# Writing the experts' leaky ReLU twice from the bank with ScalarE's parametric ReLU

## The chip, the cores and the metric

The kernel runs on one core of a Trainium2 chip. That core has TensorE (PE in the profile, with its weight loads as PEld), VectorE (DVE), ScalarE (ACT), GpSimd (POOL) and SyncE (SP), each with a queue of its own that it works through in order. The metric is the device time of one execution in microseconds, the median of several runs.

## The reference

Two stages follow each other. Attention over 8 batches, 8 heads, 576 positions and 64 dimensions mixes a causal softmax with a memory read by a gate per head. Its output, 4608 tokens of 512 features, then goes through one feed-forward layer ("the experts" below) with 2048 hidden features and a leaky ReLU:

```python
def _moe_ref(x, w_in, w_out):
    h = x @ w_in
    g = np.maximum(0.01 * h, h)
    return (g @ w_out).astype(np.float32)
```

The weights come as float64, the tokens as float32.

## The kernel before, in words

The work is cut into 16 chunks of tokens: 8 batches, each as a first chunk of 320 positions and a second of 256. For each chunk `attention` runs once for each of the 8 heads and leaves the chunk's tokens in `xh` and `xl`; `Moe` then works on the whole chunk while the attention of the next chunk runs.

The matrix products of the experts are made of float32r parts. A float32 tile is split into a high part, rounded to float32r by writing it into a float32r tile, and a low part, the rest. A product is then three matmuls: high times high, high times low, low times high. So the hidden tile needs both parts, `gh` and `gl`.

`Moe.step(f)` handles the slice f of 128 hidden features (16 slices a chunk). `first(f)` fills the one PSUM bank `h` with 12 matmuls (L620), then makes `g`, `gh` and `gl`:

- L646: ScalarE reads the bank and writes `g` = 0.01 h (scaled copy).
- L651: VectorE reads the bank and `g` and writes `g` = max(h, 0.01 h). The bank is free after this.
- L655: ScalarE copies `g` into the float32r tile `gh` (the cast).
- L660: GpSimd writes `gl` = `g` - `gh`.

`second(f-1)` adds 12 matmuls (L620 as well) of the previous slice's `gh` and `gl` to the four banks `acc`. There is one buffer of `h`, one of `g`, two each of `gh` and `gl`. After 16 slices ScalarE copies the four banks out (L693) and SyncE stores them.

The order of every queue is set by a planner (`Plan.issue`): a list schedule with fixed costs per kind of instruction (`act`, `dve`, `pool_`, `pe`), a latency between engines and a priority. Attention has the better priority on TensorE, so the experts' matmuls (priority `MOE`) fill the rest; the steps from bank to `gl` have the best priority (-1) on their engines. Each step waits for those that wrote what it reads and for those that used its buffer before. A changed cost or dependence moves the order on all queues.

The start is different. The first two chunks' attention runs in plain float32. During the first there are no experts yet; during the second the first chunk's experts run, and most of the 32 weight tiles are converted from float64 bits: ScalarE takes the magnitude (L287) and casts (L306), VectorE or GpSimd applies the lower bound (L290), VectorE does three bit operations (L293, L298, L301), GpSimd the low part (L309). From the third chunk on, attention uses the memory that the staging of the weights leaves (`late`).

Names of attention that come up below: `s` are scores (L472, L476), L480 the masked scores with their running minimum, L496 the exponential, L501, L506 and L509 the normalising of a row block `pp`, L526 its transposition into a bank `t`, L541 and L544 the copies out of it, L584 the product with v, L590 the sum that gives `x`, L512 the memory part on GpSimd.

Of the kernel before, what the change touches and what calls it, by code (L numbers as in the profile page):

```python
# [15 lines left out]
AF = mybir.ActivationFunctionType  # L16
ALU = mybir.AluOpType
# [13 lines left out]
TILES = ((0, 1, 2), (3, 4))  # L31
NJ = (3, 5)
RAWW = (320 + 320 + 3 * 64 + 64 + 3 * 64, 256 + 576 + 5 * 64 + 64 + 2 * 64)
# per q tile: rows, first column in its chunk, keys
ROWS = (64, 128, 128, 128, 128)
COL = (0, 64, 192, 0, 128)
KEYS = (64, 192, 320, 448, 576)
# score pieces per q tile: (first key, computed keys, used keys)
PIECES = (((0, 192, 64),), ((0, 192, 192),), ((0, 320, 320),), ((0, 448, 448),), ((0, 320, 320), (320, 256, 256)))
# blocks of keys per q tile that are transposed into one bank  # L40
BLOCKS = (((0, (0,)),), ((0, (0, 1)),), ((0, (0, 1)), (2, (2,))), ((0, (0, 1, 2, 3)),), ((0, (0, 1, 2)), (3, (3, 4))))
# chunks at the start whose attention runs in plain float32, while TensorE waits for the other engines
PLAIN = 2
# the first rows of the weights stay beside the first chunk, the others come into its memory
NFA = 12
# staging tiles of the weights
WR = 2
TA = {"stageA": 2, "stageB": 3}
NEG = -1.0e30


ENGINES = ("PE", "ACT", "DVE", "POOL", "DMA")
# from the end of a step to the start of one that needs it, by the engines
LATENCY = {"PE": 200, "ACT": 130, "DVE": 130, "POOL": 90, "DMA": 2000}


# [4 lines left out]


class Buf:
    """A tile that gets its memory when the first instruction on it is emitted."""

    def __init__(self, plan, pool, shape, dtype, tag, bufs, name, after):
        self.make = lambda: pool().tile(shape, dtype, tag=tag, bufs=bufs, name=name)
# [16 lines left out]


class Plan:
    """Lists the program's steps with what they read and write, then issues them engine by engine in
    the order that a list schedule over the engines gives."""

    def __init__(self):  # L90
        self.ops, self.rings, self.writers, self.readers = [], {}, {}, {}
# [90 lines left out]
def act(n, psum=False):  # L182
    return (51 if psum else 94) + 0.8333 * n


def dve(n):
    return 69 + 1.042 * n
# [10 lines left out]
def moe_attention(ctx, tc, raw0, raw1, beta, w_in, w_out, out, nb):  # L198
    nc = tc.nc
# [6 lines left out]
    plan = Plan()  # L206
    op = plan.op

    # Memory that is used in turn: by the weights' staging beside the first chunk's attention and then
    # the second's, and by what the later chunks need.  # L210
    regions, members = {}, {n: [] for n in ("stageA", "c0", "wtsB", "stageB", "c1", "late")}
    behind = {n: [] for n in members}
    behind["wtsB"] = [members["stageA"], members["c0"]]
# [27 lines left out]
    def bank(tag, bufs, name):  # L241
# [7 lines left out]
        out=mask[:, S - P :], in_=mask[:, S - P :], pattern=[[-1, P]], compare_op=ALU.is_ge, fill=NEG, base=0, channel_multiplier=1  # L249
    )  # L250
    gate = cst.tile([P, 2, H], F32, name="gate")
    # 1 / g and 1 / (1 - g) of the gate g = 1 / (1 + exp(-beta))
    braw = cst.tile([P, H], F32, name="braw")
    nc.sync.dma_start(braw, beta)
    for k in range(2):
# [19 lines left out]
    def load_weight(src, f, hi, lo, key, where, prio):  # L275
        k = f"{key}{f}"
        tile = in_turn(where)
        wr = tile([P, DM, 2], I32, "wr" + where, WR, "wr" + k)
        ta = tile([P, DM], I32, "ta" + where, TA[where], "ta" + k)

        def ld():
            nc.sync.dma_start(wr(), src[f].rearrange("p (c t) -> p c t", t=2))

        # float64 bits to float32: the high word's magnitude stays at or over that of 2 ** -127, whose
        # bits become a zero
        def mag():
            nc.scalar.activation(out=ta().bitcast(F32), in_=wr()[:, :, 1].bitcast(F32), func=AF.Abs)  # L287

        def least():
            (nc.vector if f % 2 else nc.gpsimd).tensor_scalar(out=ta().bitcast(F32), in0=ta().bitcast(F32), scalar1=floor, scalar2=None, op0=ALU.max)  # L290

        def low():
            nc.vector.tensor_scalar(  # L293
                out=ta(), in0=ta(), scalar1=0x07FFFFFF, scalar2=3, op0=ALU.bitwise_and, op1=ALU.logical_shift_left
            )

        def top():
            nc.vector.scalar_tensor_tensor(out=ta(), in0=wr()[:, :, 1], scalar=-0x40000000, in1=ta(), op0=ALU.bitwise_and, op1=ALU.bitwise_or)  # L298

        def tail():  # L300
            nc.vector.scalar_tensor_tensor(  # L301
                out=ta(), in0=wr()[:, :, 0], scalar=29, in1=ta(), op0=ALU.logical_shift_right, op1=ALU.bitwise_or
            )

        def hi_():
            nc.scalar.copy(hi(), ta().bitcast(F32))  # L306

        def lo_():
            nc.gpsimd.tensor_tensor(out=lo(), in0=ta().bitcast(F32), in1=f32r_bits(hi()), op=ALU.subtract)  # L309

        op("DMA", 3.3 * DM, prio, ld, w=[wr[0], wr[1]])
        op("ACT", act(DM), prio, mag, r=[wr[1]], w=[ta[0]])
        op(*(("DVE", 69 + 0.52 * DM) if f % 2 else ("POOL", 130 + 2.6 * DM)), prio, least, w=[ta[0]])
        op("DVE", 69 + 0.52 * DM, prio, low, w=[ta[0]])
        op("DVE", dve(DM), prio, top, r=[wr[1]], w=[ta[0]])
        op("DVE", dve(DM), prio, tail, r=[wr[0]], w=[ta[0]])
        op("ACT", act(DM), prio, hi_, r=[ta[0]], w=[hi[0]])
        op("POOL", pool_(DM), prio, lo_, r=[ta[0], hi[0]], w=[lo[0]])
# [24 lines left out]
    def attention(b, hf, h, prio):  # L343
# [17 lines left out]
        if full:  # L361
            if hf:
                pt = c1_tile([P, 1, 1216], F32, "ptc1", 2, "pt" + u)
            else:
                pt = c0_tile([P, 1, 832], F32, "ptc0", 2, "pt" + u)
        else:
            # the transposed tiles stay where they are: the columns 1024..1087 are zeros throughout
            pt = plan.buf(None, None, None, "pt", 2, None, behind["late"])
            pt.make = lambda at=pt.at: pt_tile(at % 2)
        w = ni * D  # L370
# [30 lines left out]
            op("POOL", pool_(nq), prio, q_lo, r=[raw[0], qk["q"]], w=[qk["ql"]])  # L401
            op("POOL", pool_(nk), prio, k_lo, r=[raw[0]], w=[qk["k"]])

        # phi of q over its product with z
        def ph3():
            return ph()[:, :w].rearrange("p (i d) -> p i d", d=D)

# [36 lines left out]
            op("ACT", act(nj * D), prio, v_hi, r=[raw[0]], w=[vt["h"]])  # L444
            op("POOL", pool_(nj * D), prio, v_lo, r=[raw[0], vt["h"]], w=[vt["l"]])

        # slot j holds the transposed block of keys 128j-64..128j+63; the last slot only its last 192 columns
        def cols(j, c):
            if full and not hf:
                return j * nq + c - (P if j == 2 else 0)  # L450
# [2 lines left out]
        for ii, i in enumerate(tl):  # L453
            rw, n = ROWS[i], KEYS[i]
# [10 lines left out]
            for k, (k0, kc, kn) in enumerate(PIECES[i]):  # L465
                s = bank(("acc0", "s", "acc1")[i] if (b, hf) == (0, 0) else "s", 1, f"s{u}_{i}_{k}")

                def score(s=s, i=i, k0=k0, kc=kc, kn=kn, rw=rw):
                    if full or i == 0:
                        # q and k stand on both halves of the rows: their product is twice the score  # L470
                        q, k = raw()[:, COL[i] : COL[i] + rw], raw()[:, nq + k0 : nq + k0 + kn]
                        nc.tensor.matmul(s()[:rw, :kn], q, k, start=True, stop=True)  # L472
                        return
                    for k in range(2):
                        c = COL[i] + k * (nq + nk)
                        nc.tensor.matmul(s()[:, :kc], qk()[:, c : c + P], qk()[:, nq + k0 : nq + k0 + kc], start=k == 0, stop=k == 1)  # L476

                def top(s=s, i=i, k=k, k0=k0, kn=kn, rw=rw, pp=pp, stat=stat):
                    mo = S - KEYS[i] + k0 if i else S - P
                    nc.vector.tensor_tensor_reduce(  # L480
                        out=pp()[:rw, D + k0 : D + k0 + kn],
                        in0=s()[:rw, :kn],
                        in1=mask[:rw, mo : mo + kn],
                        scale=-0.0625 if full or i == 0 else -0.125,
                        scalar=stat(k - 1) if k else 3.0e38,
                        op0=ALU.add,
                        op1=ALU.min,
                        accum_out=stat(k),
                    )

                op("PE", 4 * 0.4167 * kn if full or i == 0 else 2 * pe(kc), prio, score, r=[raw[0]] if i == 0 else operands, w=[s[0]])
                op("DVE", 80 + 1.042 * kn, prio, top, r=[s[0], st["m", ii, k - 1]], w=[pp["s", k], st["m", ii, k]])
# [116 lines left out]
    class Moe:  # L609
# [15 lines left out]
        def first(self, f, prio):  # L625
            n, u = self.n, f"{self.b}_{self.hf}_{f}"
# [3 lines left out]
            for d in range(4):  # L630
# [12 lines left out]
            gh = tile_([P, 320], F32R, "gh", 2, "gh" + u)  # L643
            gl = tile_([P, 320], F32R, "gl", 2, "gl" + u)
            q = -1
            op("ACT", act(n, True), q, lambda: nc.scalar.activation(out=g()[:, :n], in_=hp()[:, :n], func=AF.Copy, scale=0.01), r=[hp[0]], w=[g[0]])  # L646
            op(
                "DVE",
                dve(n),
                q,  # L650
                lambda: nc.vector.tensor_tensor(out=g()[:, :n], in0=hp()[:, :n], in1=g()[:, :n], op=ALU.max),  # L651
                r=[hp[0]],
                w=[g[0]],
            )
            op("ACT", act(n), q, lambda: nc.scalar.copy(gh()[:, :n], g()[:, :n]), r=[g[0]], w=[gh[0]])  # L655
            op(
                "POOL",
                pool_(n),
# [123 lines left out]
```

## Time and profile before

| | |
|---|---|
| device time, median of 3 runs | 1301.19 us (1300.96 to 1301.51) |
| span of the profiled execution | 1298.5 us |
| median less span (what lies around the span) | 2.7 us |
| TensorE busy | 1243.6 us (96%) |
| VectorE busy | 951.5 us (73%) |
| ScalarE busy | 837.7 us (65%) |
| GpSimd busy | 796.8 us (61%) |
| mean granted TensorE clock | 0.993 |

The profiled execution's own time is the span; the median of the runs is 2.7 us above it. Rows of groups read: line, engine, operation, tiles and shapes, count, then busy time and the mean of one instruction in ns, then the idle time of the engine just before them with what ended it. "A <- B: 8.7, 7, 1.8" among the waits says that A's engine sat idle 8.7 us in all, in 7 pieces, the longest 1.8 us, until B was done. The end of a matmul in the records is modelled: matmuls follow each other at a shorter distance than their shown length, so a short pause on TensorE shows only in part as idle time.

### The profile page before, as it was taken

How to read it: one execution, taken by the hardware profiler on the slowest of the kernel's cores; microseconds unless marked ns; L12 is line 12 of the kernel's file. 1: busy time of each engine (PE TensorE's matmuls, PEld its weight loads, DVE VectorE, ACT ScalarE, POOL GpSimd, SP SyncE). 2: the span in 40 equal slices, each digit the busy share in tenths (PEclk: the TensorE clock that was granted, in tenths of full speed). 3: DMA queues.
4: the chain of work that ended last, by engine and by line, in shares of the span. 5: the costliest groups of instructions: out<-in, count | busy, mean ns of one | idle time of the engine just before them, and what ended most of it. 6: DMA issues, size and time to landing. Idle time of an engine off the chain costs nothing.

```text
span 1298.5 us, 26483 instructions
## 1 busy us (share of the span) xinstructions
PE 1243.6 (96%) x8896; PEld 1159.7 (89%) x8896; DVE 951.5 (73%) x3131; ACT 837.7 (65%) x2395; POOL 796.8 (61%) x1152
## 2 busy tenths in 40 slices
PE   7778889999999999999999999999999999999998
PEld 4566779999899999999999999999999999999998
DVE  7999877877788866778578785787767776777311
ACT  7656667766777766767576765667666675776322
POOL 4687757666666665756566665666657575666222
PEclk9899999999999999999999999999999999999999
DMA  6444422212222222222122221222221221212000
GB/s 240 156 145 152 152 74 70 98 68 74 91 82 93 66 70 77 80 88 70 38 96 84 79 70 51 87 69 90 70 74 69 87 79 41 98 65 81 1 21 17
DMA packets 32535, 107.61 MB, mean 83 GB/s; under 512 B 3728, under 2 KB 11920, under 8 KB 32400
## 3 DMA queue, kind: packets, MB, share of 16 engines
q1 hardware_dynamic: 32400, 105.92, 24.1%
q8 instruction: 71, 1.16, 0.4%
q14 instruction: 64, 0.52, 0.1%
HBM read 96.47 MB, written 9.44 MB: 82 GB/s over the span
## 4 chain that ended last, share of the span: by engine, by line
PE 69%; DVE 16%; POOL 6%; issue 5%; ACT 3%; DMA 0%; POOLq 0%; SPq 0%; ACTq 0%; DVEq 0%
PE h L620 24%; PE acc L620 24%; PE t L526 7%; PE o L584 6%; PE s L476 5%; DVE pp L509 3%; DVE pp L480 2%; PE s L472 2%; POOL gl L660 2%; DVE g L651 1%; ACT pp L496 1%; POOL qk L381 1%; DVE tawi L298 1%; DVE pt L544 1%; DVE tawo L298 1%
## 5 line engine op out<-in xcount | busy, mean ns | idle before, releaser
L620 PE MATMUL h<-xh,wih 128*128 128x256 f32 (+1 forms) x1024 | 321.4, 314 | 7.8 <-DVE g L651 6.0
L660 POOL TENSOR_TENSOR gl<-g,gh 128x320 fp32r<-128x320 f32 (+1 forms) x256 | 214.0, 836 | 184.3 <-ACT gh L655 158.1
L620 PE MATMUL acc<-gh,woh 128*128 128x256 f32 (+1 forms) x1024 | 321.1, 314 | 0.3
L620 PE MATMUL h<-xl,wih 128*128 128x256 f32 (+1 forms) x1024 | 302.6, 296 | 0.9 <-DVE xl L571 0.9
L620 PE MATMUL acc<-gl,woh 128*128 128x256 f32 (+1 forms) x1024 | 302.3, 295 | 0.9 <-POOL gl L660 0.8
L620 PE MATMUL h<-xh,wil 128*128 128x256 f32 (+1 forms) x1024 | 302.2, 295 | 0.0
L620 PE MATMUL acc<-gh,wol 128*128 128x256 f32 (+1 forms) x1024 | 301.5, 294 | 0.0
L496 ACT ACTIVATE pp<-pp,st 128x448 f32<-128x448 f32 (+3 forms) x320 | 180.4, 564 | 67.6 <-DVE st L480 61.9
L651 DVE TENSOR_TENSOR g<-h,g 128x320 f32<-128x320 f32 (+1 forms) x256 | 115.9, 453 | 135.2 <-ACT g L646 133.6
L646 ACT ACTIVATE g<-h 128x320 f32<-128x320 f32 (+1 forms) x256 | 104.7, 409 | 163.6 <-PE h L620 142.3
L620 PEld LDWEIGHTS h<-xh,wih 128*128 128x128 f32 x1024 | 193.4, 189 | 18.1 <-DVE g L651 10.9
L620 PEld LDWEIGHTS acc<-gh,woh 128*128 128x128 f32 x1024 | 193.0, 188 | 7.2 <-ACT os L693 1.5
L541 ACT CAST pt<-t 128x256 fp32r<-128x256 f32 (+4 forms) x392 | 141.1, 380 | 87.4 <-PE t L526 83.0
L620 PEld LDWEIGHTS acc<-gl,woh 128*128 128x128 f32 x1024 | 193.2, 189 | 3.8 <-POOL gl L660 1.8
L620 PEld LDWEIGHTS h<-xl,wih 128*128 128x128 f32 x1024 | 193.9, 189 | 2.5 <-DVE xl L571 1.5
L526 PE MATMUL t<-ident,pp 128*128 128x128 f32 (+1 forms) x960 | 168.1, 277 | 26.5 <-DVE pp L509 11.6
L620 PEld LDWEIGHTS h<-xh,wil 128*128 128x128 f32 x1024 | 193.2, 189 | 0.0
L620 PEld LDWEIGHTS acc<-gh,wol 128*128 128x128 f32 x1024 | 192.6, 188 | 0.0
L509 DVE TENSOR_SCALAR pp<-pp,st 128x448 f32<-128x448 f32 (+3 forms) x320 | 187.7, 587 | 5.5
L544 DVE TENSOR_TENSOR pt<-t,pt 128x256 fp32r<-128x256 f32 (+4 forms) x392 | 160.0, 426 | 31.2 <-ACT pt L541 28.7
L480 DVE CUSTOM_DVE_ANT_0 pp<-s,mask 128x448 f32<-128x448 f32 (+3 forms) x320 | 136.6, 428 | 47.7 <-PE t L526 23.0
L512 POOL TENSOR_TENSOR pp<-ph,st 128x64 f32<-128x64 f32 (+1 forms) x320 | 102.1, 324 | 107.7 <-DVE st L434 50.3
(63 smaller groups left out, 2252.9 us busy)
## 6 DMA issues: line engine op xcount, KB each, us to landing
raw<-raw SPq DMA_DIRECT2D x64, 672.0 KB, 4.0
raw<-raw SPq DMA_DIRECT2D x64, 544.0 KB, 3.6
wrwi<-w_in_bits SPq DMA_DIRECT2D x16, 512.0 KB, 3.5
wrwo<-w_out_bits SPq DMA_DIRECT2D x16, 512.0 KB, 3.3
out_t<-os SPq DMA_DIRECT2D x32, 160.0 KB, 1.8
out_t<-os SPq DMA_DIRECT2D x32, 128.0 KB, 1.7
braw<-beta_b SPq DMA_DIRECT2D x1, 4.0 KB, 1.6
```

The costliest lines, as they stand in the source:

```text
L480: nc.vector.tensor_tensor_reduce(out=pp()[:rw, D + k0 : D + k0 + kn], in0=s()[:rw, :kn], in1=mask[:rw, mo : mo + kn], scale=-0.0625 if ful ...
L496: nc.scalar.activation(out=pp()[:rw, D : D + n], in_=pp()[:rw, D : D + n], func=AF.Exp, scale=-1.0, bias=stat(kl_), accum_out=stat(2))
L509: nc.vector.tensor_scalar(out=pp()[:rw, D : D + n], in0=pp()[:rw, D : D + n], scalar1=stat(2), scalar2=None, op0=ALU.mult)
L512: nc.gpsimd.tensor_tensor(out=pp()[:rw, :D], in0=ph3()[:rw, ii, :], in1=rn()[:rw, ii : ii + 1].to_broadcast([rw, D]), op=ALU.mult)
L526: nc.tensor.transpose(t()[:, (j - j0) * rw : (j - j0 + 1) * rw], pp()[:rw, j * P : (j + 1) * P], ident[:rw, :rw])
L541: nc.scalar.copy(part(0), tv())
L544: nc.vector.tensor_tensor(out=part(1), in0=tv(), in1=f32r_bits(part(0)), op=ALU.subtract)
L584: nc.tensor.matmul(o()[:, c0[j] : nq], vt()[:, j, :], pt()[:, t, cols(j, c0[j]) : cols(j, nq)], start=n == 0, stop=n == len(mm) - 1)
L620: nc.tensor.matmul(dst(), l(), r(), start=start and k + j == 0, stop=stop and k + j == len(ops) - 1)
L646: op("ACT", act(n, True), q, lambda: nc.scalar.activation(out=g()[:, :n], in_=hp()[:, :n], func=AF.Copy, scale=0.01), r=[hp[0]], w=[g[0]])
L651: lambda: nc.vector.tensor_tensor(out=g()[:, :n], in0=hp()[:, :n], in1=g()[:, :n], op=ALU.max),
L660: lambda: nc.gpsimd.tensor_tensor(out=gl()[:, :n], in0=g()[:, :n], in1=f32r_bits(gh()[:, :n]), op=ALU.subtract),
```

## The change

Two instructions of ScalarE take the place of ScalarE's scaled copy, VectorE's maximum and ScalarE's cast. Both read the bank `h` and apply the parametric ReLU with a slope of 0.01 for negative values; the first writes the float32r tile `gh`, the second the float32 tile `g`. GpSimd's subtraction stays. The bank is now free after the second write. `gh` no longer depends on `g`. The first write needs a free buffer of `gh` (two) and the second the one buffer of `g`. The planner's cost of each is that of a read from a bank, `act(n, True)`. The diff also drops comments, so line numbers shift: L660 of before is L653 of the change.

```diff
-            op("ACT", act(n, True), q, lambda: nc.scalar.activation(out=g()[:, :n], in_=hp()[:, :n], func=AF.Copy, scale=0.01), r=[hp[0]], w=[g[0]])
-            op(
-                "DVE",
-                dve(n),
-                q,
-                lambda: nc.vector.tensor_tensor(out=g()[:, :n], in0=hp()[:, :n], in1=g()[:, :n], op=ALU.max),
-                r=[hp[0]],
-                w=[g[0]],
-            )
-            op("ACT", act(n), q, lambda: nc.scalar.copy(gh()[:, :n], g()[:, :n]), r=[g[0]], w=[gh[0]])
+            op("ACT", act(n, True), q, lambda: nc.scalar.activation(out=gh()[:, :n], in_=hp()[:, :n], func=AF.Prelu, alpha=0.01), r=[hp[0]], w=[gh[0]])
+            op("ACT", act(n, True), q, lambda: nc.scalar.activation(out=g()[:, :n], in_=hp()[:, :n], func=AF.Prelu, alpha=0.01), r=[hp[0]], w=[g[0]])
```

In numbers of instructions: ScalarE keeps 2076 rows, VectorE goes from 3131 to 2875 (256 fewer), the other queues keep theirs.

The first place is VectorE where the first experts run beside the conversion of the weights (`tawi`, `tawo` are weight tiles in conversion, `pp` and `st` belong to attention). Before:

```order
L298 SCALAR_TENSOR_TENSOR tawi_625<-wrwi_564,tawi_625 128x512
L651 TENSOR_TENSOR g_0_0_690<-h_0_0_429,g_0_0_690 128x320
L301 SCALAR_TENSOR_TENSOR tawi_625<-wrwi_564,tawi_625 128x512
L290 TENSOR_SCALAR tawo_694<-tawo_694 128x512
L428 TENSOR_REDUCE st_1_0_713<-pz_1_0_586 128x2
L293 TENSOR_SCALAR tawo_694<-tawo_694 128x512
L431 TENSOR_SCALAR st_1_0_713<-st_1_0_713,gate 128x2
L480 ISA pp_1_0_3_731,st_1_0_713<-s_1_0_3_0_607,mask 128x448
L480 ISA st_1_0_713 128x1
L298 SCALAR_TENSOR_TENSOR tawo_694<-wrwo_667,tawo_694 128x512
L651 TENSOR_TENSOR g_0_1_737<-h_0_1_701,g_0_1_737 128x320
L301 SCALAR_TENSOR_TENSOR tawo_694<-wrwo_667,tawo_694 128x512
```

And of the change, from the same first row on:

```order
L298 SCALAR_TENSOR_TENSOR tawi_625<-wrwi_564,tawi_625 128x512
L301 SCALAR_TENSOR_TENSOR tawi_625<-wrwi_564,tawi_625 128x512
L290 TENSOR_SCALAR tawo_697<-tawo_697 128x512
L293 TENSOR_SCALAR tawo_697<-tawo_697 128x512
L428 TENSOR_REDUCE st_1_0_725<-pz_1_0_586 128x2
L298 SCALAR_TENSOR_TENSOR tawo_697<-wrwo_667,tawo_697 128x512
L431 TENSOR_SCALAR st_1_0_725<-st_1_0_725,gate 128x2
L480 ISA pp_1_0_3_741,st_1_0_725<-s_1_0_3_0_607,mask 128x448
L480 ISA st_1_0_725 128x1
L301 SCALAR_TENSOR_TENSOR tawo_697<-wrwo_667,tawo_697 128x512
```

The two maxima (L651) are gone and the bit operations on the weights close up; the second tile's L298 stands ahead of the scores now.

The second place is ScalarE at the same point of the program. Before:

```order
L646 ACTIVATE g_0_0_690<-h_0_0_429 128x320
L287 ACTIVATE tawo_694<-wrwo_667 128x512
L655 CAST gh_0_0_699<-g_0_0_690 128x320
L306 CAST wih_711<-tawi_625 128x512
L418 ACTIVATE pz_1_1_721<-raw_1_1_145 128x128
L287 ACTIVATE tawi_726<-wrwi_677 128x512
L646 ACTIVATE g_0_1_737<-h_0_1_701 128x320
L496 ACTIVATE pp_1_0_3_731,st_1_0_713<-pp_1_0_3_731,st_1_0_713 128x448
L287 ACTIVATE tawo_749<-wrwo_692 128x512
L655 CAST gh_0_1_756<-g_0_1_737 128x320
```

Of the change:

```order
L647 ACTIVATE gh_0_0_690<-h_0_0_429 128x320
L648 ACTIVATE g_0_0_694<-h_0_0_429 128x320
L287 ACTIVATE tawo_697<-wrwo_667 128x512
L306 CAST wih_705<-tawi_625 128x512
L287 ACTIVATE tawi_723<-wrwi_677 128x512
L418 ACTIVATE pz_1_1_732<-raw_1_1_145 128x128
L647 ACTIVATE gh_0_1_734<-h_0_1_701 128x320
L648 ACTIVATE g_0_1_743<-h_0_1_701 128x320
L496 ACTIVATE pp_1_0_3_741,st_1_0_725<-pp_1_0_3_741,st_1_0_725 128x448
L287 ACTIVATE tawo_773<-wrwo_692 128x512
```

The cast stood one to three rows behind the scaled copy, with other work put between them; the two writes now stand side by side (at 241 of the 256 slices in the whole program), ahead of the exponential.

The third place is ScalarE in the last chunk, where only experts are left. Before:

```order
L646 ACTIVATE g_1_13_18431<-h_1_13_18413 128x256
L655 CAST gh_1_13_18443<-g_1_13_18431 128x256
L646 ACTIVATE g_1_14_18463<-h_1_14_18445 128x256
L655 CAST gh_1_14_18475<-g_1_14_18463 128x256
L646 ACTIVATE g_1_15_18495<-h_1_15_18477 128x256
```

Of the change:

```order
L647 ACTIVATE gh_1_13_18178<-h_1_13_18162 128x256
L648 ACTIVATE g_1_13_18183<-h_1_13_18162 128x256
L647 ACTIVATE gh_1_14_18209<-h_1_14_18193 128x256
L648 ACTIVATE g_1_14_18214<-h_1_14_18193 128x256
L647 ACTIVATE gh_1_15_18240<-h_1_15_18224 128x256
```

The order is the same slice by slice, and both rows of a slice read its bank. In both programs the order of ScalarE holds one load of an activation table, at its first row (L256).

## The prediction

> **What bounds the kernel now.** I read the page's busy times first, then the busy times by stretch, then the waits of TensorE in each stretch, because the share over the whole span hides that the stages have different limits.
>
> ```profile
> PE 1243.6 (96%) x8896; PEld 1159.7 (89%) x8896; DVE 951.5 (73%) x3131; ACT 837.7 (65%) x2395; POOL 796.8 (61%) x1152
> ```
>
> Over the span TensorE is the bound, at 96%. The next table has one row a stretch: its limits, its length, then busy us of PE, PEld, DVE, ACT and POOL with the instructions in brackets, then the granted clock, the DMA share and GB/s.
>
> ```profile
> 0.00:50.00 50.00, 38.28 (x155) 21.38 (x155) 41.99 (x178) 34.54 (x120) 26.57 (x48) 0.97 0.57 205
> 50.00:175.00 125.00, 102.02 (x555) 81.92 (x555) 120.11 (x261) 72.88 (x166) 89.81 (x81) 0.95 0.41 142
> 175.00:200.00 25.00, 23.63 (x176) 21.59 (x174) 16.82 (x66) 18.37 (x57) 17.19 (x27) 1.00 0.29 94
> 200.00:1200.00 1000.00, 986.49 (x7311) 943.19 (x7309) 752.35 (x2579) 680.88 (x1977) 638.36 (x964) 1.00 0.23 76
> 1200.00:1298.50 98.50, 93.16 (x708) 91.59 (x706) 20.27 (x53) 30.99 (x77) 24.84 (x33) 1.00 0.04 13
> ```
>
> From 50 to 175 us it is VectorE: busy 120.1 of 125 us (96%), with TensorE idle for 23.0. From 200 on TensorE is idle for 13.5 of 1000 us, and for 5.3 of the last 98.5. So a lighter VectorE is worth most in the start, little in the middle, and at the end only what it shortens in a chain. TensorE's work does not change, so the gain is the TensorE idle time that goes away.
>
> What TensorE waits for from 50 to 175 us (us in total, times, longest):
>
> ```profile
> PE t L526 <- DVE pp L509: 8.7, 7, 1.8
> PE s L472 <- DVE st L480: 6.4, 5, 2.2
> PE h L620 <- DVE g L651: 2.4, 1, 2.4
> ```
>
> 17.5 of the 23.0 us end with VectorE: twice attention's steps stood in its full queue, and once the bank of the experts was held by the maximum.
>
> **The change part by part: the price of an instruction.** The groups by shape over the whole run (busy us, mean ns of one):
>
> ```profile
> L651 DVE TENSOR_TENSOR g<-h,g 128x320 f32<-128x320 f32 x128 | 62.3, 487 | 78.4 <-ACT g L646 77.7
> L655 ACT CAST gh<-g 128x320 fp32r<-128x320 f32 x128 | 58.9, 460 | 35.6 <-DVE g L651 33.4
> L646 ACT ACTIVATE g<-h 128x320 f32<-128x320 f32 x128 | 55.8, 436 | 92.2 <-PE h L620 88.7 <-POOL pp L512 1.4 <-POOL qk L381 0.7
> L646 ACT ACTIVATE g<-h 128x256 f32<-128x256 f32 x128 | 48.9, 382 | 71.4 <-PE h L620 53.6 <-POOL gl L660 15.8 <-PE acc L620 1.0
> L541 ACT CAST pt<-t 128x256 fp32r<-128x256 f32 x168 | 62.0, 373 | 47.9 <-PE t L526 46.0
> L496 ACT ACTIVATE pp<-pp,st 128x320 f32<-128x320 f32 x64 | 36.1, 565 | 2.6 <-DVE st L480 2.2
> ```
>
> No parametric ReLU stands in this trace. The nearest row is L646: the same bank, shape and engine, with an immediate scale. Writing float32r from a bank costs no more (L541: 373 ns against L646's 382 at 256 columns). The dearest form of an activation at 320 columns is the exponential with a bias per row, 565. I take L646's price for both writes and keep 565 as the upper end. ScalarE then loses 128 x (460 - 436) ns = 3 us and about as much at the narrower shape, 6 us of 838; at the upper end it gains 512 x 129 ns = 66 less 6, to 898 us or 69% of the span, still far from the bound. VectorE loses 256 maxima.
>
> [...]
>
> **Start (50 to 175 us).** How much of VectorE's queue a maximum takes is seen in its starts, since consecutive instructions overlap a little:
>
> ```profile
> 106.03 0.48 DVE L651 TENSOR_TENSOR g<-h,g 128x320 f32<-128x320 f32 x1
> 106.43 0.28 DVE L421 SCALAR_TENSOR_TENSOR ph<-ph,pz 128x128 f32<-128x128 f32 x1
> ...
> L651 DVE TENSOR_TENSOR g<-h,g 128x320 f32<-128x320 f32 x15 | 7.2, 483 | 2.5 <-ACT g L646 2.3
> L655 ACT CAST gh<-g 128x320 fp32r<-128x320 f32 x15 | 6.9, 457 | 9.5 <-DVE g L651 9.5
> ```
>
> The last two rows are the groups of this stretch alone. 15 maxima at 0.40 us make 6.0 us of a queue that is 96% full. ScalarE also stops standing for 9.5 us before its casts with other work behind it; it has room there (73 of 125 us), so I count nothing for that. Not all 6.0 us need reach the end, for each weight tile also passes ScalarE and GpSimd, the latter 90 of 125 us busy. I take 5.0. The ends are 0, if another engine holds the start, and 8.4, if the 2.4 us wait for the bank goes as well.
>
> **Middle (200 to 1200 us).** The waits of TensorE that VectorE ends, then the maxima in the two halves (length, busy us, count):
>
> ```profile
> PE t L526 <- DVE pp L509: 2.9, 10, 0.6
> PE h L620 <- DVE g L651: 1.5, 6, 0.3
> PE t L526 <- DVE x L590: 1.4, 5, 0.3
> PE t L526 <- DVE st L501: 1.0, 2, 0.7
> PE s L476 <- DVE st L480: 0.8, 2, 0.6
> PE t L526 <- DVE pt L544: 0.5, 2, 0.3
> ...
> 200.00:700.00 500.00, 46.41 (x103) 1.00 0.23 77
> 700.00:1200.00 500.00, 47.10 (x105) 1.00 0.23 75
> ```
>
> That is 8.1 us in 27 waits, and 93.5 us of maxima, 12% of VectorE's 752. A wait costs more than it shows. The last chunk, where the chain is undisturbed, gives both this and the chain's lengths (start, length; one slice, then the last one, then copies of the banks, then twelve matmuls):
>
> ```profile
> 1288.54 0.38 ACT L646 ACTIVATE g<-h 128x256 f32<-128x256 f32 x1 [1.57 <-PE h L620]
> 1288.96 0.42 DVE L651 TENSOR_TENSOR g<-h,g 128x256 f32<-128x256 f32 x1 [2.42 <-ACT g L646]
> 1289.42 0.41 ACT L655 CAST gh<-g 128x256 fp32r<-128x256 f32 x1 [0.49 <-DVE g L651]
> 1289.90 0.74 POOL L660 TENSOR_TENSOR gl<-g,gh 128x256 fp32r<-128x256 f32 x1 [2.11 <-ACT gh L655]
> ...
> 1292.73 0.38 PE L620 MATMUL acc<-gh,woh 128*128 128x256 f32 x1
> 1293.53 0.38 PE L620 MATMUL acc<-gl,woh 128*128 128x256 f32 x1 [0.42 <-POOL gl L660]
> ...
> 1294.48 1.02 ACT os L693 x3
> ...
> 1244.61 1.40 PE h L620 x12
> ```
>
> Matmuls follow at 1.40 / 12 = 0.12 us. The wait shown as 0.42 pushed the next start 0.80 back, so it cost 0.68, 0.26 more than shown. The 27 waits then cost about 8.1 + 7.0 = 15.1 us.
>
> The chain: the bank was free at 1289.38, 0.84 us after the first read began. Two reads in a row on ScalarE start about 0.32 apart ((1.02 - 0.38) / 2), so the second ends 0.70 after: 0.14 earlier. `gh` is ready at 0.38 and not 1.29 (0.91 earlier), and `gl` can start at 0.77 instead of 1.36 (0.59 earlier).
>
> So the six waits for the bank give 6 x 0.14 = 0.8 us. Of the other 21, with 6.6 + 5.5 = 12.1 us, I take 30%, 3.6: more than the 12% by which the queue shrinks, since delay in a queue falls faster than its load, and not all, since these steps also wait for ScalarE. Together 4.4. The ends are 0, if the planner's new order makes as many waits of its own, and 15.1.
>
> **End (1200 us on).** The waits of TensorE in this stretch are two of each kind:
>
> ```profile
> PE h L620 <- DVE g L651: 0.9, 2, 0.6
> PE acc L620 <- POOL gl L660: 0.8, 2, 0.4
> ```
>
> The two for `gl` shrink by 0.59 each, the two for the bank by 0.14: 1.5 us. At the dear price of a write (0.13 more each) `gl` would come 0.33 earlier and the bank 0.12 later: 0.4.
>
> **Sum.** 5.0 + 4.4 + 1.5 = 10.9 us. The profiled span of 1298.5 becomes 1287.6; the median of the runs lies 2.7 above the span, so 1290.3. What hides the unpriced parts is TensorE's own work: behind each slice of `h` stand 12 matmuls of `acc`, 1.40 us or more, and the bank is needed again only after them, against 0.70 for both writes.
>
> **The rivals.** First, another owner of the start. If the conversion is held by the path through GpSimd (72% busy) and ScalarE, the 6.0 us on VectorE turn into idle time there. Against it stand VectorE's 96% and the 17.5 of 23.0 us. Left are 0.8 + 1.5 = 2.3 us: 1298.9, within 0.2%, which is 2.6 us and about what can be told from no change here. Chance 0.13.
>
> Second, slower: ScalarE holds the bank. Its queue is in order, and the second write needs `g`'s one buffer back from GpSimd.
>
> ```profile
> ACT g L646 <- POOL gl L660: 15.8, 12, 1.8
> L496 ACT ACTIVATE pp<-pp,st 128x576 f32<-128x576 f32 x64 | 49.8, 779 | 21.9 <-DVE st L480 21.2
> ```
>
> Both uses of the bank now stand behind whatever ScalarE has in front of them, an exponential of 779 ns or a wait for `gl` of up to 1.8 us. It decides when the release comes later than the 1.40 us that 12 matmuls cover, so when the pair is held up by more than 0.70. If that cost 0.3 us at a quarter of the 256 slices, it is 19 us, and with the gains 8 us net: 1309. Against it: the scaled copy stood in the same queue and waited for the same buffer, and ScalarE is 68% busy in the middle. Chance 0.08.
>
> Third, the change doesn't do what it says: the engine cannot hold the exponential and the parametric ReLU ready together and loads a table at each turn between them.
>
> ```profile
> L256 ACT ACT_TABLE_LOAD x1 | 1.3, 1283 | 0.7 <-PEq L766 0.7
> ```
>
> Two loads a slice would be 512 x 1.283 = 657 us, and ScalarE with 832 + 657 = 1489 us would be the bound: about 1490 or more. Against it, the order of the changed program shows one load, as before. Chance 0.01. [...]
>
> **How the numbers follow.** The forecast, with a real gain in the start, has 0.78; its own range is 1284 (8.4 in the start, half of the 15.1 in the middle and 1.5, about 17 us) to 1297 (half of the 6.0, then 0.8 and 0.4, about 4). Faster by over 0.2% is this case, 0.78; within 0.2% the first rival, 0.13; slower the other two, 0.09. Perhaps 0.05 of the forecast lies below 1284. The range of 1284 to 1300.5 takes in the first rival and leaves out 0.05 and 0.09.
>
> **What would show it.** Right: VectorE's busy time down by 7.2 us in the start and 93.5 in the middle; ScalarE near 832 over the span, its two new rows at 436 and 382; ScalarE no longer standing for VectorE ahead of `gh`; TensorE's idle time before 200 us down by about 5 us, and the point where it stays full as much earlier; each last-chunk wait for `gl` 0.6 us shorter. Wrong: idle time of TensorE before 200 us as before with GpSimd or ScalarE fuller there (first rival); waits of `h` for ScalarE of some us in total in the middle (second); more than one table load (third); writes well over 436 ns, which would cut the end's term first.

## The result, and the profile after

The changed kernel takes 1313.86 us (median of 4 runs, 1313.09 to 1314.91), the kernel before beside it 1301.35 (1300.96 to 1302.36). The ratio is 1.0092 with an interval of 1.0080 to 1.0104: slower by 0.9%, 12.5 us, where 10.9 us of gain were forecast. The profiled span is 1311.3 us.

The busy times of the page first:

```profile
PE 1242.4 (95%) x8896; PEld 1162.0 (89%) x8896; DVE 891.7 (68%) x2875; ACT 823.1 (63%) x2395; POOL 795.4 (61%) x1152
```

TensorE has the same work and stands idle for 68.9 us of the span, not 54.9. The busy times by stretch, in the columns of the prediction, say where:

```profile
0.00:50.00 50.00, 38.29 (x155) 21.29 (x155) 42.08 (x178) 34.55 (x120) 26.86 (x48) 0.97 0.58 202
50.00:175.00 125.00, 104.42 (x573) 85.27 (x572) 114.83 (x245) 72.65 (x168) 92.81 (x83) 0.95 0.43 143
175.00:200.00 25.00, 23.74 (x182) 22.00 (x180) 17.17 (x67) 18.84 (x59) 17.44 (x28) 1.00 0.29 94
200.00:1200.00 1000.00, 970.78 (x7210) 929.75 (x7210) 701.57 (x2340) 659.99 (x1949) 623.57 (x948) 1.00 0.23 75
1200.00:1311.30 111.30, 105.19 (x784) 103.69 (x783) 16.10 (x50) 37.04 (x100) 34.73 (x45) 0.98 0.05 18
```

Up to 200 us TensorE did 166.45 us of work (38.29 + 104.42 + 23.74) against 163.93 before: the start gained 2.5. From 200 to 1200 it is idle for 29.2 us, where it was 13.5. At 1200 us 105.19 us of its busy time are left, against 93.16. Not all of that is more work, for the granted clock of this stretch is 0.98 where it was 1.00: behind a wait of 1.6 us for a copy out of the banks two slices of 10 us have a lower clock.

```profile
1260.00:1270.00 10.00, 8.24 (x58) 7.63 (x57) 0.00 (x0) 2.17 (x6) 1.52 (x3) 0.89 0.15 51
1270.00:1280.00 10.00, 10.00 (x82) 10.00 (x82) 0.00 (x0) 2.64 (x8) 2.23 (x4) 0.94 0.00 0
```

By an estimate from those two clocks, (0.11 + 0.06) x 10 = 1.7 us of the 105.19 come from it, so some 103.5 stand against 93.16. TensorE came 2.5 ahead into the middle and leaves it 10.3 behind: the middle lost about 13 us. The rest of the 12.8 us by which the span grew, about 2.5, was lost in the last stretch. Busy time stands for work here, which is good to some 3 us; the first `acc` matmuls of the chunks say the same, 3.3 us ahead at the second chunk (180.4 us against 183.7), 9.4 behind at the fifteenth (1192.7 against 1183.3) and 12.7 at the end.

The waits of TensorE in the middle (us in total, times, longest):

```profile
PE t L526 <- DVE pp L509: 22.8, 42, 1.1
PE h L620 <- ACT g L648: 3.2, 5, 0.6
PE o L584 <- DVE pt L544: 0.9, 1, 0.9
```

Before, transpositions waited 2.9 us for L509 and the experts' matmuls 1.5 for their bank. L509 is VectorE's multiplication of a row block of probabilities by its scale, in place in SBUF, which L526 then transposes. The change does not touch it. The groups by shape, of the new lines and of two steps of VectorE that the change leaves alone (busy us, mean ns):

```profile
L647 ACT ACTIVATE gh<-h 128x320 fp32r<-128x320 f32 x128 | 55.8, 436 | 98.3 <-PE h L620 97.6
L648 ACT ACTIVATE g<-h 128x320 f32<-128x320 f32 x128 | 55.5, 433 | 1.6 <-PE h L620 1.5
...
L421 DVE SCALAR_TENSOR_TENSOR ph<-ph,pz 128x128 f32<-128x128 f32 x64 | 45.2, 706 | 7.5 <-ACT pz L418 7.1
L509 DVE TENSOR_SCALAR pp<-pp,st 128x320 f32<-128x320 f32 x64 | 44.2, 690 | 1.2
...
L509 DVE TENSOR_SCALAR pp<-pp,st 64x64 f32<-64x64 f32 x64 | 25.2, 394 | 1.3
```

The same groups of before:

```profile
L509 DVE TENSOR_SCALAR pp<-pp,st 128x320 f32<-128x320 f32 x64 | 36.0, 562 | 1.3
...
L421 DVE SCALAR_TENSOR_TENSOR ph<-ph,pz 128x128 f32<-128x128 f32 x64 | 30.0, 469 | 3.8 <-ACT pz L418 3.1
...
L509 DVE TENSOR_SCALAR pp<-pp,st 64x64 f32<-64x64 f32 x64 | 24.2, 379 | 1.1
```

The writes cost what was forecast. At the shapes shown L421 (two operands in SBUF) became 706 ns from 469 and L509 690 from 562. Not every shape of L509 got longer (128x448 went from 728 to 657); over all its shapes the mean rose from 587 to 611. Two places in the changed kernel show what stretches L509 (start, length; around 500 and around 520 us, each time GpSimd's rows, then L509, then TensorE's):

```profile
499.84 0.29 POOL L512 TENSOR_TENSOR pp<-ph,st 64x64 f32<-64x64 f32 x1 [1.12 <-issue]
500.09 0.73 POOL L653 TENSOR_TENSOR gl<-g,gh 128x256 fp32r<-128x256 f32 x1
500.79 0.85 POOL L596 TENSOR_TENSOR xl<-x,xh 128x320 fp32r<-128x320 f32 x1
...
500.00 1.82 DVE L509 TENSOR_SCALAR pp<-pp,st 128x320 f32<-128x320 f32 x1
...
501.97 0.41 PE L526 MATMUL t<-ident,pp 128*128 128x128 f32 x2 [1.00 <-DVE pp L509]
...
520.42 1.41 POOL L381 TENSOR_TENSOR qk<-raw,qk 64x576 fp32r<-64x576 f32 x1
...
520.55 1.34 DVE L509 TENSOR_SCALAR pp<-pp,st 64x64 f32<-64x64 f32 x1
...
522.03 0.24 PE L526 MATMUL t<-ident,pp 64*128 64x64 f32 x1 [0.73 <-DVE pp L509]
```

The shortest L509 of this trace took 0.24 us; the 64x64 one at 520.55, beside GpSimd's L381, took 1.34 and ended 0.06 us after it. The one at 500.00 ended 0.18 us after the third of three GpSimd instructions. The rest of the trace bears this out. Of the 64 multiplications of 64x64, the 29 with no GpSimd instruction beside them took 239 to 248 ns, and the 35 with one took 517 in the mean and up to 1339; at the other four shapes, too, none without one took over 520. In both places the transposition starts 0.15 us behind the end of L509, and TensorE, whose queue is in order, stands idle for 1.00 and 0.73 us before it. The program repeats every two chunks, and so do these waits; the two of TensorE's rows above come again 154.84 and 154.85 us later, with two more of their kind:

```profile
656.81 0.41 PE L526 MATMUL t<-ident,pp 128*128 128x128 f32 x2 [0.99 <-DVE pp L509]
676.88 0.24 PE L526 MATMUL t<-ident,pp 64*128 64x64 f32 x1 [0.73 <-DVE pp L509]
687.68 0.52 PE L526 MATMUL t<-ident,pp 128*128 128x128 f32 x3 [0.33 <-DVE pp L509]
697.37 0.52 PE L526 MATMUL t<-ident,pp 128*128 128x128 f32 x3 [0.78 <-DVE pp L509]
```

Such holds are not new: between 200 and 1200 us the trace shows 29 multiplications of over 1 us before and 31 after. Their number hardly changed, so the likelier difference is which they are and what stands right behind them on TensorE. That is set by the planner's order, which no line of the diff shows.

### The profile page after: what moved, and what is told of

Its sections match the earlier page's. It is cut to its first block, busy times and chain, and to the rows that moved or that the text cites. A ratio compares the mean times of both kernels' runs of the same rounds, so it can differ in the third digit from the quotient of the medians.

```text
span 1311.3 us, 26037 instructions
## 1 busy us (share of the span) xinstructions
PE 1242.4 (95%) x8896; PEld 1162.0 (89%) x8896; DVE 891.7 (68%) x2875; ACT 823.1 (63%) x2395; POOL 795.4 (61%) x1152
## 4 chain that ended last, share of the span: by engine, by line
PE 69%; DVE 17%; ACT 8%; issue 3%; POOL 2%; DMA 1%; POOLq 0%; SPq 0%; DVEq 0%; ACTq 0%
PE h L620 25%; PE acc L620 24%; PE t L526 7%; PE o L584 6%; DVE pp L509 6%; PE s L476 5%; ACT pp L496 3%; DVE pp L480 2%; PE s L472 2%; DVE ph L421 1%; DVE pt L544 1%; ACT g L648 1%; ACT gh L647 1%; ACT qk L377 1%; DVE tawi L301 1%
## 5 line engine op out<-in xcount | busy, mean ns | idle before, releaser
L653 POOL TENSOR_TENSOR gl<-g,gh 128x320 fp32r<-128x320 f32 (+1 forms) x256 | 212.3, 829 | 185.7 <-ACT g L648 173.7
L496 ACT ACTIVATE pp<-pp,st 128x448 f32<-128x448 f32 (+3 forms) x320 | 180.4, 564 | 72.5 <-DVE st L480 67.4
L647 ACT ACTIVATE gh<-h 128x320 fp32r<-128x320 f32 (+1 forms) x256 | 104.8, 409 | 168.0 <-PE h L620 163.6
L526 PE MATMUL t<-ident,pp 128*128 128x128 f32 (+1 forms) x960 | 170.2, 277 | 39.4 <-DVE pp L509 32.4
L509 DVE TENSOR_SCALAR pp<-pp,st 128x448 f32<-128x448 f32 (+3 forms) x320 | 195.4, 611 | 7.1
L544 DVE TENSOR_TENSOR pt<-t,pt 128x256 fp32r<-128x256 f32 (+4 forms) x392 | 161.2, 428 | 50.8 <-ACT pt L541 47.8
L512 POOL TENSOR_TENSOR pp<-ph,st 128x64 f32<-128x64 f32 (+1 forms) x320 | 98.5, 314 | 143.6 <-DVE st L434 61.3
L526 PEld LDWEIGHTS t<-ident,pp 128*128 128x128 f32 (+1 forms) x960 | 113.9, 141 | 67.5 <-POOL gl L653 9.8
```

The lines of the kernel that those rows point to most:

```text
L496: nc.scalar.activation(out=pp()[:rw, D : D + n], in_=pp()[:rw, D : D + n], func=AF.Exp, scale=-1.0, bias=stat(kl_), accum_out=stat(2))
L509: nc.vector.tensor_scalar(out=pp()[:rw, D : D + n], in0=pp()[:rw, D : D + n], scalar1=stat(2), scalar2=None, op0=ALU.mult)
L512: nc.gpsimd.tensor_tensor(out=pp()[:rw, :D], in0=ph3()[:rw, ii, :], in1=rn()[:rw, ii : ii + 1].to_broadcast([rw, D]), op=ALU.mult)
L526: nc.tensor.transpose(t()[:, (j - j0) * rw : (j - j0 + 1) * rw], pp()[:rw, j * P : (j + 1) * P], ident[:rw, :rw])
L544: nc.vector.tensor_tensor(out=part(1), in0=tv(), in1=f32r_bits(part(0)), op=ALU.subtract)
L653: lambda: nc.gpsimd.tensor_tensor(out=gl()[:, :n], in0=g()[:, :n], in1=f32r_bits(gh()[:, :n]), op=ALU.subtract),
```

## The experiments

**Theory 1:** the loss comes from the new order of the queues, not from the new instructions. It sets L509 beside GpSimd's instructions, which hold it, with the transposition close behind. **Theory 2 (rival):** the two new writes cost the time in any order. **Theory 3 (rival):** the order counts, but only because transpositions stand too close behind L509; GpSimd has no part.

Each run is given as its median and its ratio to the kernel before on the same chip. In several runs a step of the plan issues nothing: it takes part in the ordering as if it were an instruction.

**The old order with parametric ReLU.** One write from the bank takes the scaled copy's place, the maximum stays in the plan without an instruction, the cast stays:

```diff
-            op("ACT", act(n, True), ... out=gh()[:, :n], in_=hp()[:, :n], func=AF.Prelu, alpha=0.01), r=[hp[0]], w=[gh[0]])
             op("ACT", act(n, True), ... out=g()[:, :n], in_=hp()[:, :n], func=AF.Prelu, alpha=0.01), r=[hp[0]], w=[g[0]])
+            op("DVE", dve(n), q, lambda: None, r=[hp[0]], w=[g[0]])
+            op("ACT", act(n), q, lambda: nc.scalar.copy(gh()[:, :n], g()[:, :n]), r=[g[0]], w=[gh[0]])
```

> The plan of before is kept slot by slot: ScalarE's parametric ReLU writes g in the place of the scaled copy, the maximum keeps its slot in the plan but issues nothing, the cast of g into gh stays. Every queue has the order of before, less VectorE's 256 maxima. Theory 1 (the loss came with the planner's new order, which sets the normalising L509 on VectorE beside GpSimd's instructions and the transposition close behind it): 1290 to 1299 us, with TensorE's waits for L509 near the 11.6 us of before. Theory 2 (the loss comes from the new instructions themselves, whatever the order): 1306 us or more.

Measured: 1291.57 us, 0.9916 (0.9899 to 0.9932). Its stretches and its waits in the middle:

```profile
0.00:200.00 200.00, 167.04 (x905) 128.66 (x906) 173.85 (x488) 127.79 (x348) 136.51 (x159) 0.96 0.45 152
200.00:1200.00 1000.00, 986.47 (x7343) 947.27 (x7342) 691.74 (x2381) 678.70 (x1983) 637.67 (x967) 1.00 0.24 76
1200.00:1290.30 90.30, 85.42 (x654) 84.17 (x652) 2.54 (x7) 25.98 (x66) 21.73 (x28) 0.99 0.04 14
```

```profile
PE t L526 <- DVE pp L509: 1.2, 3, 0.4
```

Without the maxima and in the old order the kernel is faster by 0.8%, about 11 us, and TensorE waits for L509 for 1.2 us of the middle instead of 22.8, although 22 multiplications of the middle still take over 1 us. But this run has one write from the bank and a cast, not two writes. The next has both.

**The change's two instructions in the old order.** Both writes are issued in the scaled copy's place, the maximum's and the cast's places issue nothing. For this `gh` has three buffers instead of two, and a probability tile of the second chunk is cut to 512 columns to make room:

```diff
+            gh.make = lambda: sb.tile([P, 320], F32R, tag="gh", bufs=3, name="gh" + u)
...
+            op("ACT", act(n, True), q, both_writes, r=[hp[0]], w=[g[0]])
+            op("DVE", dve(n), q, lambda: None, r=[hp[0]], w=[g[0]])
+            op("ACT", act(n), q, lambda: None, r=[g[0]], w=[gh[0]])
```

> The change's two writes from the bank, both, in the order of before: the plan of before decides, both writes are issued in the slot of the scaled copy, the slots of maximum and cast issue nothing. Since gh is now written earlier than the plan thinks, it has a third buffer; the second chunk's row block of 448 keys is cut to the columns it uses to make room. Theory 1: as with the cast kept, 1288 to 1295 us, so the two instructions are worth about 10 us and all of the loss is the order's. Rival (the second read of the bank or the early gh costs on its own): 1298 us or more.

Measured: 1292.72 us, 0.9925 (0.9904 to 0.9945).

```profile
PE t L526 <- DVE pp L509: 1.5, 4, 0.6
```

The rows of TensorE and of GpSimd stand in the order of before in the traces of both runs, so the old order was kept. Theory 2 falls: the two writes bring 0.75% where the order stays. With the same two instructions the change's order costs 1.0092 / 0.9925 = 1.0168, about 22 us.

**A third order.** The change with the maximum left in the plan, but without an instruction:

```diff
+            op("DVE", dve(n), q, lambda: None, r=[hp[0]], w=[g[0]])
```

> The instructions of the change, but the plan still holds a maximum on VectorE behind the two writes (issuing nothing), so it believes VectorE as full and the bank as long held as before. Theory 1: another order that leaves L509 more room, 1295 to 1306 us, waits of TensorE for L509 under 20 us. Theory 2: 1308 us or more. Should it be above 1310 with the waits for L509 at 30 us, then any new order costs as much and the lighter VectorE in the plan is not what did it.

Measured: 1304.7 us, 1.0014 (1.0004 to 1.0024).

```profile
PE t L526 <- DVE pp L509: 12.0, 24, 1.1
```

Another order, another time: the same two writes took 1292.7, 1304.7 and 1313.9 us in three orders (0.9925, 1.0014 and 1.0092 of the kernel before). The waits for L509 rise in the same order, 1.5, 12.0 and 22.8 us; the next runs ask how much of the time is theirs.

**The change's order with L509 in another form.** L509 also sums its row (into an unused column). Below this is the summing form, and the form of before the plain (or fast) one. With no GpSimd instruction beside it the plain form is the faster: at 128x576 509 to 520 ns in the change, against 801 to 812 here. No plan price changes, so the order stays:

```diff
-                nc.vector.tensor_scalar(... scalar1=stat(2), scalar2=None, op0=ALU.mult)
+                nc.vector.tensor_scalar(... scalar1=stat(2), scalar2=0.0, op0=ALU.mult, op1=ALU.add, accum_out=stat(3))
```

> The change in its own order, but L509 also writes the sum of its row, which keeps it from the fast form. [...] Theory 1: L509 gets shorter though its form is slower (0.25 to 0.75 us by shape, none near 1.8 us), TensorE's waits for it fall from 32.4 to under 12 us, 1294 to 1303 us. Theory 3 (the transposition simply stands too close behind L509 in the order, GpSimd has no part in it): L509's mean rises or stays, the waits stay, 1309 us or more.

Measured: 1289.39 us, 0.9898 (0.9879 to 0.9917). That is more gain than expected. TensorE is idle for 12.7 us of the middle, not 29.2. Its waits for L509 there, then the groups of L509 over all shapes:

```profile
PE t L526 <- DVE pp L509: 2.1, 5, 0.8
```

```profile
L509 DVE TENSOR_SCALAR_CACHE_REDUCE pp<-pp,st 128x448 f32<-128x448 f32 (+3 forms) x320 | 173.1, 541 | 7.1
...
L509 DVE DVE_READ_ACCUMULATOR pp<-pp,st 128x1 f32 (+1 forms) x320 | 25.7, 80 | 0.0
```

One form replaced in the same order takes back 1.9%, some 25 us. The two instructions together are no shorter than the one (541 + 80 ns against a mean of 611), but none takes over 815 ns, where the other form took up to 1819, and the write that the transposition waits for comes earlier. GpSimd no longer matters to it: at 64x64 the 26 with no GpSimd instruction beside them took 259 to 273 ns, the 38 with one 257 to 272. No earlier run had shown that, nor the 0.25 to 0.75 us of the expectation, which were my estimate; by shape the means are 267 to 810 ns.

**Controls for the form.** The same edit in the kernel before, in the old order with parametric ReLU, and in the third order:

> The kernel before, with its own order, and L509 in the form that also writes the sum of its row. A control for the gain of that form without the change. Theory 1 (L509 in the fast form is held while GpSimd works, and the change's order makes that worse): the form is worth less here, where TensorE waited 11.6 us for L509 and not 32.4: 1293 to 1300 us. If it is worth about 25 us here too (1277 or less), the form is simply a better one and says nothing on the change's order.

> The parametric ReLU in the place of scaled copy and maximum, cast kept, in the order of before, and L509 in the row-sum form. Theory 1: both gains nearly add, 1284 to 1290 us. Rival: TensorE is full in the middle either way, no more than 2 us under 1291.6.

> The order of the run with the phantom maximum in the plan (1304.7 us with the fast L509), with L509 in the row-sum form. Theory 1: the form is worth more than the 9.8 us that it was worth in the order of before, since TensorE waited 19.6 us for L509 there against 11.6: 1285 to 1294 us. Rival (the form is worth the same in every order): 1294.5 to 1297 us.

Measured: before 1291.73 us, 0.9921 (0.9905 to 0.9937); old order 1279.24 us, 0.9831 (0.9809 to 0.9853); third order 1292.17 us, 0.9918 (0.9901 to 0.9934). The first two gained more than expected, the third lies in the expected range. So the form is worth 0.8% in the kernel before, 0.9% in the old order (0.9831 against 0.9916), 1.0% in the third and 1.9% in the change's. Part of what the run in the change's order took back is thus a gain that any order has. The third order is no support for theory 1: TensorE waited 12.0 us for L509 there, and yet the form brings no more, within the intervals, than in the old order. Against the old order with a cast the third costs 1.0014 / 0.9916 = 1.0099 with the plain form and still 0.9918 / 0.9831 = 1.0088, about 11 us, with the summing one. So nearly all of its price comes from something else. With this form the change's order costs 0.9898 / 0.9831 = 1.0068, about 9 us, instead of 22: some 13 us of the order's price, give or take 5 by the intervals, hang on the plain form of L509. The old order with this form is the fastest full version of the study, 1.7% under the kernel before:

```profile
200.00:1200.00 1000.00, 991.35 (x7404) 956.10 (x7403) 684.15 (x2646) 680.11 (x1984) 627.95 (x965) 1.00 0.23 76
```

**GpSimd shortened, L509 in the plain form.** In the change's order GpSimd's L381 works on 64 columns only, so most of the low part of k is left out:

```diff
-            ks = slice(nq, nq + nk)
+            ks = slice(nq, nq + 64)
```

> The change in its own order and with the fast form of L509, but GpSimd's L381 works on 64 columns of k and not on 320 or 576, so it leaves out the low part of most of k. GpSimd loses its longest instructions, some 100 of 795 us. Theory 1: fewer and shorter holds of L509; its waits on TensorE fall from 32.4 to about 15 to 24 us and the time to 1298 to 1307 us. Theory 3 (GpSimd has no part in it): waits as before and 1310 us or more.

Measured: 1291.11 us, 0.9918 (0.9901 to 0.9935). Waits in the middle, then two groups over all shapes:

```profile
PE t L526 <- DVE pp L509: 9.1, 13, 1.1
```

```profile
L509 DVE TENSOR_SCALAR pp<-pp,st 128x448 f32<-128x448 f32 (+3 forms) x320 | 165.8, 518 | 7.1
...
L421 DVE SCALAR_TENSOR_TENSOR ph<-ph,pz 128x128 f32<-128x128 f32 (+1 forms) x128 | 62.0, 485 | 30.7 <-ACT pz L418 29.6 <-ACT ph L415 0.2
```

Theory 3 falls: neither L509 nor the order was touched, and L509 went from 611 to 518 ns, L421 from 656 to 485, and TensorE's waits for L509 from 22.8 to 9.1. The gain, 23 us, was larger than I had expected (1298 to 1307 us). The edit also takes some 93 us of work from GpSimd (L381 130.1 us to 37.2), so not all of it need be holds.

**Truer prices in the plan.** The plan prices L509 at 430 ns for 576 columns, and the trace shows 800 to 869. Here L509 and L421 have prices nearer to the trace. (The 728 ns of the expectation is what the trace of before has at 448 columns; at 576 it has 800, and L421 has 469 at 128 columns, not 384.)

```diff
-            op("DVE", dve2(n) + 40, prio, scale, ...
+            op("DVE", 250 + 0.83 * n, prio, scale, ...
...
-        op("DVE", dve(w), prio, phi_add, ...
+        op("DVE", 256 + w, prio, phi_add, ...
```

> The change, with the planner's price of L509 and L421 raised to what the trace of before measured (at 576 columns 728 in place of 430 ns, L421 at 128 columns 384 in place of 202). Theory 1: the plan keeps transpositions further behind L509, its waits fall to under 20 us, 1296 to 1306 us. Theory 2: 1309 us or more.

Measured: 1301.9 us, 1.0002 (0.9990 to 1.0013). The waits over the whole span:

```profile
PE s L472 <- DVE st L480: 13.1, 15, 2.4
PE t L526 <- DVE pp L509: 9.7, 14, 1.5
```

In the middle it helped as meant (TensorE busy 983.6 us of 1000, waits for L509 5.0), but that order has other stalls; of the first row 11.9 us lie in the first 200 us. There the granted clock was also 0.94, as in the third order with the plain form, against 0.96 in the kernel before and the change, which is worth an estimated 4 us (0.02 x 200). These don't account for all of its time, and I did not settle where the rest goes. So waits for L509 alone don't set the time of an order. With the summing form and prices for it the same idea gave the following.

> The change with L509 in the row-sum form and the plan's prices of L509 (at 576 columns 750 ns) and L421 set to that. Theory 1: with no long L509 left a new order is harmless, 1284 to 1294 us, against 1301.9 for the raised prices with the fast form. Rival (every new order of this planner loses by itself): 1299 us or more.

Measured: 1291.03 us, 0.9912 (0.9893 to 0.9932). That is no better than the unpriced order with this form (1289.39).

**The last hold: L421.** Beside GpSimd it is slow as well: at 128x128 in the change the 9 with no GpSimd instruction beside them took 268 to 284 ns, the 55 with one 775 in the mean and up to 1509. It reads two tiles. Here it reads one, as a minimum that also sums its row, and the positive part is left out; L509 sums too. First in the change's order, then in the old one:

```diff
-            nc.vector.scalar_tensor_tensor(out=ph()[:, :w], in0=ph()[:, :w], scalar=1.0, in1=pz()[:, :w], op0=ALU.min, op1=ALU.add)
+            nc.vector.tensor_scalar(out=ph()[:, :w], in0=ph()[:, :w], scalar1=1.0, scalar2=0.0, op0=ALU.min, op1=ALU.add, accum_out=st()[:, 23:24])
```

> The order of the change with L509 in the row-sum form (1289.4 us), and L421 reduced to a minimum with 1 that reads one tile, with row sum; it leaves out adding the positive part to phi. Whether holds of L421, which read two tiles and averaged 686 ns at 128 columns, are the rest of the order's loss. If they are: 1281 to 1285 us, at least 4 us more gain than the same edit brings in the order of before. If not: 1286 us or more, and no more gain than there.

> The control for the run before: the same two edits in the order of before with the parametric ReLU and the cast (1279.2 us with the row-sum L509 alone). It leaves out adding the positive part to phi as well. If holds of L421 are the rest of the order's loss: 1277 to 1280 us, less gain than in the order of the change. If not: the same gain in both.

Measured: 1279.34 us, 0.9822 (0.9805 to 0.9838), and 1274.77 us, 0.9780 (0.9762 to 0.9799). Both lie below the expected ranges. L421's mean at 128x128 is 276 and 273 ns there. The edit is worth 0.76% in the change's order and 0.51% in the old one; the difference, about 3 us, lies within the intervals, so it is not settled that L421's holds are a part of what the order costs. What is left between the two orders is 0.9822 / 0.9780 = 1.0043, 5.5 us.

## Why the prediction was wrong

**The step that failed** is the middle term: 4.4 us, with 0 as its lower end "if the planner's new order makes as many waits of its own". The order made far more: the middle lost about 13 us, and in the old order the same two instructions gain. So the lower end of 0 had no ground. I had taken re-planning as noise around the old order. What the runs showed in its place is a price of the new order of about 22 us, of which some 13, give or take 5, hang on the plain form of L509, whose holds TensorE waits out (22.8 us of waits in the middle, where it had 2.9). For these waits the prediction named VectorE's load and ScalarE, and asked neither what stood beside VectorE's steps on GpSimd nor what stood behind them on TensorE. The trace of before could have warned me: this row, from the view of one line's instructions (shortest, median, longest in ns), shows a multiplication of known size taking from 235 to 1616 ns.

```profile
L509 DVE TENSOR_SCALAR pp<-pp,st x320: 235/506/1616, 9.2 to 1208.2; 128x448 f32<-128x448 f32 x64, 64x64 f32<-64x64 f32 x32, 128x320 f32<-128x320 f32 x32, 128x192 f32<-128x192 f32 x32
```

Its shapes explain only a part: those of 64x64 had a mean of 379 against a shortest of 235. Of these 64 the 29 with no GpSimd instruction beside them took 235 to 248 ns, the 35 with one up to 1015. The runs agree: in the change's order a 64x64 multiplication beside GpSimd took up to 1339 ns in the plain form and at most 272 in the summing one. What is shown is that the holds go with that form (611 ns in the mean, where the summing one took 541), come only beside GpSimd's instructions and shrink with GpSimd's work (611 to 518 ns with L381 cut to 64 columns); what makes them was not measured.

**The sum where the order stays** was nearly right. In the old order with parametric ReLU the start gained 167.04 - 163.93 = 3.1 us (5.0 forecast), the middle 93.16 - 85.42 - 3.1 = 4.6 (4.4) and the end the remaining 0.5 of the 8.2 us of span (1.5); by the times at which the chunks' first `acc` matmuls start, it was 2.5, 4.9 and 0.9. Its 1291.57 and the 1292.72 with both writes stand beside the forecast 1290.3. With both writes the split is another one: by the same times the profiled execution, at 1296.19 us the slowest of its four, is 0.9 us behind at the end of the start, gains 5.6 in the middle and loses 0.6 at the end. So the total of the sum is borne out for these instructions, the terms of start and end are not, and what the planner would make of the change the sum did not ask.

**Start, as it ran:** 2.5 us, half the forecast, within its range. VectorE's busy time from 50 to 175 us fell by 5.3 us (7.2 forecast), and TensorE's waits for L509 there did not shrink (9.5 us, 8.7 before).

**Price and load:** 436 and 433 ns at 320 columns, as taken from the scaled copy; ScalarE 823.1 us for 832. VectorE's busy time fell by 59.8 us over the span, not by the 116 of the maxima, and by 50.8 in the middle, not 93.5. L421 (mean 656 at 128 instructions, +20 us) and L509 (+8) took 28 back. The other 26 or so are overlap: consecutive instructions overlap in the records, the lengths of all of VectorE's instructions added up fell by 86.3 us, and busy time counts what overlaps once. The start of the prediction reckoned with that (0.40 us for 0.48), the middle did not.

**End:** the waits for `gl` are gone from the last stretch as forecast, but one for the copies out of the banks came, with the lower clock behind it; instead of a gain of 1.5 us the stretch lost about 2.5:

```profile
PE acc L620 <- ACT os L686: 1.6, 1, 1.6
PE h L620 <- ACT g L648: 0.7, 1, 0.7
```

**The rivals.** The slower one, ScalarE holding the bank, gave the right sign by the wrong path: `h` waited 3.2 us for ScalarE in the middle where it waited 1.5 for VectorE, against the 19 us that the rival needed. Its 1309 was nearer to the time than the forecast, but by chance. The same-time rival did not come up, nor did the table loads: the changed kernel's trace has one, of 1.28 us.

**Open:** 5 to 9 us of the price of the change's order, and about 11 of the third order's, remain when L509 has the summing form. Whether L421's holds, the order of the start or something else makes them was not settled.

## What to carry to other kernels

Where a planner sets the order, a change of instructions is two changes. Price them apart: run the new instructions in the old order, by steps that take part in the plan and issue nothing, before judging either. Where an instruction's time ranges widely at one shape, a neighbour may hold it (64x64 took 235 to 1339 ns here): sort its times by what runs beside it, and look for what waits right behind it in an in-order queue, for there the hold becomes idle time (22.8 us of the middle here). A form that is not held can beat one that is faster alone: here 1289.39 us against 1313.86, with 801 to 812 ns against 509 to 520 at 128x576.

## What the runs showed of the hardware

- A plain multiplication on VectorE (64x64, float32, in place in SBUF) took 239 to 248 ns with no GpSimd instruction beside it and up to 1339 with one; with the sum of its row it took 257 to 273 either way.
- One plain multiplication lasted through three GpSimd instructions: the one at 500.00 us in the changed kernel ran through L512, L653 and L596 in a row, 1.82 us, where this shape took 377 to 390 ns with none beside it.
- The summing form of the multiplication had an accumulator read of 80 ns behind it, and the kernel was faster with it in all four programs that had it both ways, by 0.8 to 1.9%.
- Parametric ReLU on ScalarE cost what a scaled copy of the same shape cost, in float32r and in float32: 436 and 433 ns against 436 at 128x320, 383 and 379 against 382 at 128x256.
